# Loading fp32 weights on SyncE's queue with casts on POOL, column sums in bf16 parts, and zero rows beside a half tile

## The chip, the cores and the metric

The kernel runs on one core of one Trainium2 chip. The metric is device time in microseconds (us) of one execution. A "span" is what the profiler saw of one execution; it is about 1.8 us shorter than the device time of the same execution.

## The reference, cut to what matters

```python
B, N, C = 4, 6080, 256                     # q, k, v: (4, 6080, 256) fp32; tau = 1
qn = q / (np.linalg.norm(q, axis=1, keepdims=True) + 1e-6)
kn = k / (np.linalg.norm(k, axis=1, keepdims=True) + 1e-6)
s = kn.transpose(0, 2, 1) @ qn / tau       # (4, 256, 256): one Gram matrix a batch
a = softmax(s)                             # over the last axis
x = (v @ a).reshape(24320, 256)
h = x @ w_in                               # (256, 2048)
return gelu_tanh(h) @ w_out                # (2048, 256)
```

The kernel folds `a @ w_in` into one matrix `aw` a batch, so that each block of 512 tokens needs only `v @ aw`, the gelu, and `@ w_out`.

## The kernel before

Batch 0's attention is computed first (the head). Then 48 blocks of tokens run. Each has 8 slots of four `hp` matmuls (`aw` by transposed v), a gelu on ACT and some `yp` matmuls (`wout`). The attention of the next batch is fed into the slots, a tile of 128 tokens at a time. 6080 tokens are 47 full tiles and a half tile of 64 rows.

The weights are cast by the DMA on POOL's queue, behind a gate that holds them back until a late chunk of k has landed:

```python
# in the head, after the third chunk from the end:
        if n == n_chunks - 3:
            nc.gpsimd.tensor_copy(gate[:, 0:1], st[1][0:1, 0, 0:1])
...
    for c0, c1 in ((0, 1024), (1024, D)):
        nc.gpsimd.dma_start(out=win_bf[:, :, c0:c1], in_=win_v[:, :, c0:c1])
    load_v(1)
    for half in range(2):
        nc.gpsimd.dma_start(out=wout_bf[:, half * 8 : half * 8 + 8, :],
                            in_=wout_v[:, half * 8 : half * 8 + 8, :])
    load_v(2)
```

The Gram matmuls and the sums of squares of the later batches (cut):

```python
            for s, rows in slots_of(ch):             # rows is 64 for the half tile
                first, last = seen == 0, seen == n_all - 1
                gram(G, qk, s, rows, first, last)
                flat = whole[:rows, :, s, :]
                ...                                  # acc (fp32) += flat * flat, on DVE
                yield                                # one slot
                ...
        cols = pA.tile([128, 512], FP32, tag="a", name="cols")
        col_sums(cols, [acc[:, x] for x in range(2)], ones_f, True, True)   # 4 fp32 matmuls
```

Of the kernel before, what the change touches and what calls it, by code (L numbers as in the profile page):

```python
# [8 lines left out]
FP32 = mybir.dt.float32  # L9
BF16 = mybir.dt.bfloat16  # L10
# [8 lines left out]
def kernel(  # L19
# [10 lines left out]
    nc = tc.nc  # L30
    B, N, C = q.shape
    D = moe_w_in.shape[1]
# [8 lines left out]
    REM = N - S_ALL * 128  # L41
# [3 lines left out]
    stage = ctx.enter_context(tc.tile_pool(name="stage", bufs=4))  # L45
# [1 line left out]
    sqp = ctx.enter_context(tc.tile_pool(name="sqp", bufs=3))  # L47
    prp = ctx.enter_context(tc.tile_pool(name="prp", bufs=2))
    sq1 = ctx.enter_context(tc.tile_pool(name="sq1", bufs=4))
    accp = ctx.enter_context(tc.tile_pool(name="accp", bufs=2))  # L50
    smx = ctx.enter_context(tc.tile_pool(name="smx", bufs=2))
    awp = ctx.enter_context(tc.tile_pool(name="awp", bufs=2))
    vts = ctx.enter_context(tc.tile_pool(name="vts", bufs=4))
# [11 lines left out]
    SMAX = 6  # L65
# [11 lines left out]
    def load_chunk(engines, dst, b, chunk, step=1):  # L77

        s0, size, rem = chunk
        for x, src in enumerate((q, k)):  # L80
            engines[x].dma_start(  # L81
                out=dst[x][:, 0:size, :],
                in_=src[b, s0 * 128 : (s0 + size) * 128, :].rearrange("(p s) c -> p s c", s=size))
        if rem:
            for x, src in enumerate((q, k)):
                engines[x].dma_start(out=dst[x][0 : REM * step : step, size, :], in_=src[b, S_ALL * 128 : N, :])

    def slots_of(chunk, rest=REM):
        _, size, rem = chunk
        return [(s, 128) for s in range(size)] + ([(size, rest)] if rem else [])  # L90
# [43 lines left out]
    ones_bf = const.tile([128, 1], BF16)  # L134
    nc.vector.memset(ones_bf, 1.0)
    ones_f = const.tile([128, 1], FP32)
# [3 lines left out]
    gate = const.tile([1, 8], FP32)  # L140
# [3 lines left out]
    win_bf = const.tile([128, 2, D], BF16)  # L144
    wout_bf = const.tile([128, FC, 256], BF16)
    win_v = moe_w_in.rearrange("(c p) d -> p c d", p=128)
# [19 lines left out]
    def col_sums(cols, x, ones, first, last):  # L166

        for m in range(4):
            nc.tensor.matmul(  # L169
                cols[:, m : m + 1],  # L170
                lhsT=x[m // 2][:, m % 2 * 128 : m % 2 * 128 + 128],
                rhs=ones,
                start=first and m == 0,
                stop=last,
                skip_group_check=True,
            )
# [78 lines left out]
    for n, ch in enumerate(first_chunks):  # L255
        st, whole = staged[n]
        size = ch[1]
        qkb, qk_whole = halves(qkp, "qk", BF16, size)
        sqb, sq_whole = halves(sqp, "sq", BF16, size)
        hi = size + ch[2]  # L260
        if whole is None:
            todo = list(zip(qkb, sqb, st))
        else:
            todo = [[y[:, :, 0:hi] for y in (qk_whole, sq_whole, whole)]]
        for to, sq, x in todo:
            nc.vector.tensor_copy(to, x)  # L266
            if n != n_chunks - 2:
                nc.scalar.activation(sq, x, AF.Square)  # L268
        if n == n_chunks - 2:
            nc.scalar.activation(sqb[1][:, 0:hi], st[1][:, 0:hi], AF.Square)  # L270
            nc.vector.tensor_mul(sqb[0][:, 0:hi], qkb[0][:, 0:hi], qkb[0][:, 0:hi])
        keep_clock(fillers[n])
        for s, rows in slots_of(ch, 128):
            gram(G, qkb, s, rows, seen == 0, seen == n_all - 1)
            seen += 1
        if waiting is not None:
            pairs_of(*waiting)
            waiting = None
        if n < 2:
            pairs_of(n, sqb)  # L280
        elif n < TAIL:
            waiting = (n, sqb)
        else:
            sums_of([[y[:rows, s, :] for y in sqb] for s, rows in slots_of(ch, 128)], n == n_chunks - 1)

        for x in ((2, 3) if n == 0 else (4, 5) if n == 1 else (n + 4,)):
            stage_chunk(x)
        if n == n_chunks - 3:
            nc.gpsimd.tensor_copy(gate[:, 0:1], st[1][0:1, 0, 0:1])

    v0 = stage.tile([128, 2, SMAX, 256], FP32, tag="st", name="v0")
    v0 = v0.rearrange("p a b c -> p (a b) c")[:, 0:4, :]
# [10 lines left out]
    def load_v(nb):  # L303
        if nb >= B * n_blocks:
            return
        r0, n, rest = v_parts(nb)
        t = vin.tile([128, 4, 256], BF16, tag="v", name="vb")
        nc.gpsimd.dma_start(  # L308
            out=t[:, 0:n, :],
            in_=v_rows[r0 : r0 + n * 128, :].rearrange("(p s) c -> p s c", s=n))  # L310
        if rest:
            nc.gpsimd.dma_start(out=t[:rest, n, :], in_=v_rows[r0 + n * 128 : r0 + n * 128 + rest, :])
        v_of[nb] = t
# [21 lines left out]
    def load_qk(b, n):  # L335
        if b < B and n < len(later_chunks):
            if at_slot:
                pace()
            t = qkp.tile([128, 2, SMAX, 256], BF16, tag="qk", name="qkb")
            views = [t[:, x] for x in range(2)]  # L340
            load_chunk((nc.gpsimd, nc.gpsimd), views, b, later_chunks[n])
            loaded_of[b, n] = views, t

    for c0, c1 in ((0, 1024), (1024, D)):
        nc.gpsimd.dma_start(out=win_bf[:, :, c0:c1], in_=win_v[:, :, c0:c1])
    load_v(1)
    for half in range(2):
        nc.gpsimd.dma_start(out=wout_bf[:, half * 8 : half * 8 + 8, :],
                            in_=wout_v[:, half * 8 : half * 8 + 8, :])
    load_v(2)  # L350


    r = smx.tile([128, 4], FP32, tag="r", name="r")
# [74 lines left out]
    def attention_steps(b, aw_next):  # L428

        for n in range(16):  # L430
            if n in (3, 9):
                load_qk(b, n // 6)
            if b == 1 and n == 5:
                turn_v_on_pe(1)
            yield
        G = pA.tile([128, 2, 256], FP32, tag="a", name="G")
        acc = accp.tile([128, 2, 256], FP32, tag="acc", name="acc")
        seen = 0
        for n, ch in enumerate(later_chunks):
            load_qk(b, n + 2)  # L440
            qk, whole = loaded_of.pop((b, n))
            for s, rows in slots_of(ch):
                first, last = seen == 0, seen == n_all - 1
                gram(G, qk, s, rows, first, last)
                flat = whole[:rows, :, s, :]
                if first:
                    nc.vector.tensor_mul(acc, flat, flat)
                else:
                    sq = sq1.tile([128, 2, 256], BF16, tag="sq", name="sq")
                    nc.vector.tensor_mul(sq[:rows], flat, flat)  # L450
                    nc.vector.tensor_add(acc[:rows], acc[:rows], sq[:rows])  # L451
                seen += 1
                yield
                if seen % 8 == 0:
                    yield

        cols = pA.tile([128, 512], FP32, tag="a", name="cols")
        col_sums(cols, [acc[:, x] for x in range(2)], ones_f, True, True)
        r = smx.tile([128, 4], FP32, tag="r", name="r")
        nc.vector.tensor_copy(r, cols[:, 0:4])  # L460
        nc.gpsimd.tensor_tensor(r, r, half4, op=ALU.pow)  # L461
        yield
        yield
        yield
        norms(r)
        rh = smx.tile([128, 2], FP32, tag="rh", name="rh")
        nc.vector.tensor_scalar_mul(rh, r[:, 0:2], 0.5)
        Gs = scaled(G, r)
        yield
        yield  # L470
        T = turned(Gs)
        eT = smx.tile([128, 2, 256], BF16, tag="eT", name="eT")
        if abs(inv_tau) > TANH_MAX:
            for jc in range(2):
                nc.scalar.activation(eT[:, jc, :], T[:, jc, :], AF.Exp, scale=r[:, jc : jc + 1])
            yield
        else:
            th = smx.tile([128, 2, 256], FP32, tag="th", name="th")
            den = smx.tile([128, 2, 256], FP32, tag="den", name="den")
            for jc in range(2):  # L480
                nc.scalar.activation(th[:, jc, :], T[:, jc, :], AF.Tanh, scale=rh[:, jc : jc + 1])
            for jc in range(2):
                yield
                nc.vector.tensor_scalar(den[:, jc, :], th[:, jc, :], -1.0, 1.0,
                                        op0=ALU.mult, op1=ALU.add)
                nc.vector.reciprocal(den[:, jc, :], den[:, jc, :])
                nc.vector.scalar_tensor_tensor(
                    out=eT[:, jc, :], in0=th[:, jc, :], scalar=1.0, in1=den[:, jc, :],
                    op0=ALU.add, op1=ALU.mult)
            yield  # L490
            yield
        rsinv = row_sums(eT)
        for fs in range(D // 512):
            for ic in range(2):
                aw_part(eT, rsinv, aw_next, fs, ic)
                yield
# [159 lines left out]
```

## Time and profile before

| | before |
|---|---|
| device time, median of 4 runs | 756.50 us (756.24 to 757.38) |
| span of the profiled run | 754.2 us |
| PE busy | 733.3 us (97%) |
| first `hp` matmul (end of the head) | 41.05 us |
| first `hp` to first Gram matmul of batch 1 | 66.64 - 41.05 = 25.59 us |
| from there to the last `yp` groups | 748.80 - 66.64 = 682.16 us |

The last row comes from the PE timeline. In these views a line is: start in us, length in us, engine, source line, operation, output and inputs, shapes, and in brackets what idle time the engine had before it and what ended it. PE is TensorE and PEld its weight loads, ACT is ScalarE, DVE is VectorE, POOL is GpSimd, SPq is SyncE's queue. `G` is the Gram matrix, `eT` the exponential of its scaled transpose, and `ps` holds `eT` times `win` on its way to `aw`. The prediction shows the lines themselves.

### The profile page before, as it was taken

What the parts mean: (1) busy time and instruction counts of PE and PEld (TensorE: products, weight loads), DVE (VectorE), ACT (ScalarE), POOL (GpSimd) and SP (SyncE); (2) the same over time, 40 slices, a digit from 0 to 9 for tenths busy, and PEclk for the clock granted to TensorE, in tenths of its full rate; (3) what the DMA queues carried; (4) which work ended last, traced back from release to release, by engine and by line L of the source; (5) the groups of instructions that cost most, each with busy time, mean ns of one, the idle gap of its engine ahead of it and who ended that gap; (6) DMA issues with size and microseconds to landing.
All of it is one profiled execution on the core that took longest, in us unless ns stands there. A gap on an engine that the chain in (4) does not pass through costs nothing.

```text
span 754.2 us, 12371 instructions
## 1 busy us (share of the span) xinstructions
PE 733.3 (97%) x5262; PEld 503.5 (67%) x5262; DVE 277.5 (37%) x485; ACT 420.3 (56%) x411; POOL 75.6 (10%) x150
## 2 busy tenths in 40 slices
PE   2999999999999999999999999999999999999998
PEld 1656666776666666776666666766767666666666
DVE  3733556454401546554521265555441011011011
ACT  4875555555456555555555555555546655555552
POOL 1311111101012102101001102010101000000000
PEclk9999999999999999999999999999999999999999
DMA  9999685615147685813435776661513543322111
GB/s 368 346 190 156 103 150 137 118 43 83 48 93 143 114 161 108 162 52 60 99 57 118 140 117 121 148 133 46 83 43 80 96 95 74 69 74 54 41 56 57
DMA packets 79639, 83.59 MB, mean 111 GB/s; under 512 B 55392, under 2 KB 59104, under 8 KB 79072
## 3 DMA queue, kind: packets, MB, share of 16 engines
q0 software_dynamic: 17104, 32.97, 27.4%
q1 hardware_dynamic: 62176, 48.20, 23.8%
q10 hardware_dynamic: 304, 1.64, 0.5%
q8 instruction: 41, 0.67, 0.4%
q14 instruction: 14, 0.11, 0.0%
HBM read 78.91 MB, written 24.90 MB: 138 GB/s over the span
## 4 chain that ended last, share of the span: by engine, by line
PE 94%; DMA 4%; ACT 1%; issue 0%; DVE 0%; SPq 0%; POOL 0%; DVEq 0%
PE yp L510 44%; PE hp L584 44%; PE G L157 4%; PE ps L217 2%; ACT sq L268 1%; DMA st<-in_q_dram 1%; DMA st<-in_k_dram 1%; DMA win_bf<-in_moe_w_in_dram 1%; PE cols L169 0%; PE yp L615 0%; PE T L195 0%; DVE aw L404 0%; PE vps L422 0%; PE ps L384 0%; PE rs L204 0%
## 5 line engine op out<-in xcount | busy, mean ns | idle before, releaser
L588 ACT ACTIVATE g<-hp 128x1024 bf16<-128x1024 f32 (+1 forms) x384 | 389.8, 1015 | 308.2 <-PE hp L584 308.2
L510 PE MATMUL yp<-wout_bf,g 128*128 128x256 bf16 x3024 | 392.0, 273 | 0.0
L584 PE MATMUL hp<-vT,aw 128*128 128x512 bf16 (+1 forms) x1536 | 390.8, 377 | 0.2 <-DVE aw L404 0.2
L510 PEld LDWEIGHTS <-g 128*128 128x128 bf16 x3024 | 295.9, 98 | 113.4
L584 PEld LDWEIGHTS <-aw 128*128 128x128 bf16 x1536 | 149.9, 98 | 104.7 <-issue 0.6
L527 DVE COPY ysb<-yp 128x512 f32<-128x512 f32 (+1 forms) x95 | 64.9, 683 | 402.5 <-PE yp L510 402.5
L451 DVE TENSOR_TENSOR acc<-acc,sq 128x512 f32<-128x512 f32 (+1 forms) x141 | 97.5, 692 | 4.8
L450 DVE TENSOR_TENSOR sq<-qkb 128x512 bf16<-128x512 bf16 (+1 forms) x141 | 58.7, 417 | 0.0
L157 PE MATMUL G<-qkb 128*128 128x256 bf16 (+1 forms) x288 | 55.0, 273 | 0.0
L308 POOL DMA_DIRECT2D vb<-in_v_dram x47 | 25.8, 551 | 76.6 <-DMA vT<-vb 64.3
L226 DVE TENSOR_SCALAR aw<-ps,rsinv 128x512 bf16<-128x512 f32 x30 | 22.4, 749 | 27.1 <-PE ps L217 26.7
L157 PEld LDWEIGHTS <-qkb 128*128 128x128 bf16 (+1 forms) x288 | 27.9, 98 | 3.8 <-issue 0.6
L333 POOL CAST gate<-g 1x1 f32<-1x1 bf16 x24 | 5.9, 244 | 237.3 <-ACT g L588 237.3
L157 PE MATMUL G<-qk 128*128 128x256 bf16 x96 | 13.7, 301 | 15.6 <-DVE qk L266 15.6
L268 ACT ACTIVATE sq<-st 128x3072 bf16<-128x3072 f32 (+2 forms) x9 | 21.1, 2379 | 11.2 <-DMA st<-in_q_dram 8.2
L157 PEld LDWEIGHTS <-qk 128*128 128x128 bf16 x96 | 9.9, 108 | 19.0 <-DVE qk L266 16.6
L266 DVE CAST qk<-st 128x3072 bf16<-128x3072 f32 (+2 forms) x10 | 14.2, 1437 | 13.2 <-DMA st<-in_q_dram 10.0
L217 PE MATMUL ps<-win_bf,eT 128*128 128x512 bf16 x60 | 17.7, 379 | 0.0
L461 POOL TENSOR_TENSOR r<-r,half 128x4 f32<-128x4 f32 x3 | 3.1, 1043 | 113.8 <-DVE r L460 113.8
L81 POOL DMA_DIRECT2D qkb<-in_q_dram x24 | 12.8, 535 | 6.8 <-issue 4.7
L81 POOL DMA_DIRECT2D qkb<-in_k_dram x24 | 12.9, 538 | 0.0
L567 POOL COPY g<-gr 128x1024 bf16<-128x1024 bf16 x2 | 2.1, 1036 | 105.1 <-PE yp L510 105.1
(69 smaller groups left out, 100.7 us busy)
## 6 DMA issues: line engine op xcount, KB each, us to landing
out_dram<-ysb SPq DMA_DIRECT2D x44, 512.0 KB, 2.9
vb<-in_v_dram POOLq DMA_DIRECT2D x43, 256.0 KB, 6.8
qkb<-in_q_dram POOLq DMA_DIRECT2D x21, 384.0 KB, 4.7
qkb<-in_k_dram POOLq DMA_DIRECT2D x21, 384.0 KB, 6.5
st<-in_q_dram SPq DMA_DIRECT2D x2, 1536.0 KB, 11.8
vT<-vb SPq DMA_TRANSPOSE x184, 3.0
st<-in_k_dram ACTq DMA_DIRECT2D x1, 1536.0 KB, 10.3
st<-in_k_dram SPq DMA_DIRECT2D x1, 1536.0 KB, 16.7
```

The lines of the kernel that those rows point to most:

```text
L81: engines[x].dma_start(out=dst[x][:, 0:size, :], in_=src[b, s0 * 128 : (s0 + size) * 128, :].rearrange("(p s) c -> p s c", s=size))
L157: nc.tensor.matmul(G[:, ic, :], lhsT=qk[1][:rows, s, ic * 128 : ic * 128 + 128], rhs=qk[0][:rows, s, :], start=first and ic == 0, stop=las ...
L217: nc.tensor.matmul(ps, lhsT=eT[:, jc, ic * 128 : ic * 128 + 128], rhs=win_bf[:, jc, fs * 512 : fs * 512 + 512], start=jc == 0, stop=jc == 1)
L226: nc.vector.tensor_scalar_mul(dst, ps, scale)
L268: nc.scalar.activation(sq, x, AF.Square)
L308: nc.gpsimd.dma_start(out=t[:, 0:n, :], in_=v_rows[r0 : r0 + n * 128, :].rearrange("(p s) c -> p s c", s=n))
L450: nc.vector.tensor_mul(sq[:rows], flat, flat)
L451: nc.vector.tensor_add(acc[:rows], acc[:rows], sq[:rows])
L510: nc.tensor.matmul(yp[:rows, at, :], lhsT=g[:, fc, s * 128 : s * 128 + rows], rhs=wout_bf[:, fc, :], start=fc == 0, stop=fc == FC - 1)
L527: nc.vector.tensor_copy(ysb[:, s0 : s + 1, :], yp[:, 0 : s + 1 - s0, :])
L584: nc.tensor.matmul(hp[:, j, :cols], lhsT=aw[:, cc, fc * 128 : fc * 128 + 128], rhs=vT[:, cc, :cols], start=cc == 0, stop=cc == 1)
L588: nc.scalar.activation(g[:, 2 * i : 2 * i + 2, :cols], hp[:, :, :cols], AF.Gelu_apprx_tanh)
```

## The change

It has three parts. Weights load as plain fp32 on SyncE's queue and are cast on POOL, to let them start earlier. The sums of squares are split into three bf16 numbers that add up exactly, to avoid fp32 matmuls. The half tile gets zero rows, to make all Gram matmuls the same shape.

```diff
-        if n == n_chunks - 3:
-            nc.gpsimd.tensor_copy(gate[:, 0:1], st[1][0:1, 0, 0:1])
...
+            if later_chunks[n][2]:
+                nc.gpsimd.memset(t[REM:, :, later_chunks[n][1], :], 0.0)
             load_chunk((nc.gpsimd, nc.gpsimd), views, b, later_chunks[n])
...
-    for c0, c1 in ((0, 1024), (1024, D)):
-        nc.gpsimd.dma_start(out=win_bf[:, :, c0:c1], in_=win_v[:, :, c0:c1])
-    load_v(1)
-    for half in range(2):
-        nc.gpsimd.dma_start(out=wout_bf[:, half * 8 : half * 8 + 8, :],
-                            in_=wout_v[:, half * 8 : half * 8 + 8, :])
-    load_v(2)
+    for half in range(2):
+        w = flat_stage(2)                            # a buffer of the q/k staging pool
+        for x in range(2):
+            c0 = half * 1024 + x * 512
+            nc.sync.dma_start(out=w[:, :, x * 512 : x * 512 + 512], in_=win_v[:, :, c0 : c0 + 512])
+            nc.gpsimd.tensor_copy(win_bf[:, :, c0 : c0 + 512], w[:, :, x * 512 : x * 512 + 512])
+        load_v(1 + half)
+    for half in range(2):
+        w = flat_stage(8)
+        nc.sync.dma_start(out=w, in_=wout_v[:, half * 8 : half * 8 + 8, :])
+        nc.gpsimd.tensor_copy(wout_bf[:, half * 8 : half * 8 + 8, :], w)
...
-            for s, rows in slots_of(ch):
+            for s, rows in slots_of(ch, 128):
...
+        parts = [split.tile([128, 2, 256], BF16, tag=f"part{n}", name="part") for n in range(3)]
+        nc.vector.tensor_copy(parts[0], acc)
+        nc.vector.tensor_sub(acc, acc, parts[0])
+        nc.vector.tensor_copy(parts[1], acc)
+        nc.vector.tensor_sub(parts[2], acc, parts[1])
+        yield
+        yield
         cols = pA.tile([128, 512], FP32, tag="a", name="cols")
-        col_sums(cols, [acc[:, x] for x in range(2)], ones_f, True, True)
+        for n, part in enumerate(parts):
+            col_sums(cols, [part[:, x] for x in range(2)], ones_bf, n == 0, n == 2)
```

Left out: the accumulator's pool goes from two buffers to one, and a pool for the parts is added.

More of the change, by code (lines that the diff above doesn't have):

```diff
@@ L49 @@
     sq1 = ctx.enter_context(tc.tile_pool(name="sq1", bufs=4))
-    accp = ctx.enter_context(tc.tile_pool(name="accp", bufs=2))
+    split = ctx.enter_context(tc.tile_pool(name="split", bufs=1))
+    accp = ctx.enter_context(tc.tile_pool(name="accp", bufs=1))
     smx = ctx.enter_context(tc.tile_pool(name="smx", bufs=2))
@@ L340, in load_qk, with flat_stage @@
             views = [t[:, x] for x in range(2)]
+            if later_chunks[n][2]:
+                nc.gpsimd.memset(t[REM:, :, later_chunks[n][1], :], 0.0)
             load_chunk((nc.gpsimd, nc.gpsimd), views, b, later_chunks[n])
             loaded_of[b, n] = views, t
-    for c0, c1 in ((0, 1024), (1024, D)):
-        nc.gpsimd.dma_start(out=win_bf[:, :, c0:c1], in_=win_v[:, :, c0:c1])
-    load_v(1)
+    def flat_stage(n):
+        w = stage.tile([128, 2, SMAX, 256], FP32, tag="st", name="wst")
+        return w.rearrange("p a b c -> p (a b c)")[:, 0:2048].rearrange("p (c d) -> p c d", c=n)
     for half in range(2):
-        nc.gpsimd.dma_start(out=wout_bf[:, half * 8 : half * 8 + 8, :],
-                            in_=wout_v[:, half * 8 : half * 8 + 8, :])
-    load_v(2)
+        w = flat_stage(2)
[8 more added lines that the diff above has]
+        nc.gpsimd.tensor_copy(wout_bf[:, half * 8 : half * 8 + 8, :], w)
     r = smx.tile([128, 4], FP32, tag="r", name="r")
```

## The prediction

> **What bounds the kernel now.** I read the page from the top: span and busy shares, the slices, then the chain of work that ended last.
>
> ```profile
> span 754.2 us, 12371 instructions
> PE 733.3 (97%) x5262; PEld 503.5 (67%) x5262; DVE 277.5 (37%) x485; ACT 420.3 (56%) x411; POOL 75.6 (10%) x150
> PE   2999999999999999999999999999999999999998
> PEclk9999999999999999999999999999999999999999
> PE 94%; DMA 4%; ACT 1%; issue 0%; DVE 0%; SPq 0%; POOL 0%; DVEq 0%
> ```
>
> The reader is to see one full row. PE is busy in every slice but the first and last, its clock is full throughout, and 94% of the chain is PE. The view by stretches says it more sharply: from 50 us to 700 us PE is busy in all of every stretch. So after about 41 us a change can win only by giving PE less to do, and can lose only by making PE wait. Before that, the chain runs through loads: in order of time it is q load, squares, k load, and then this:
>
> ```profile
> 31.83 7.78 DMA win_bf<-in_moe_w_in_dram
> 41.05 1.04 PE hp L584 x4
> ```
>
> The weight load is on the path. The timeline shows by how much:
>
> ```profile
> 38.23 0.84 ACT L374 ACTIVATE eT<-T,r 128x256 bf16<-128x256 f32 x2 [0.50 <-PE T L195]
> 39.74 0.38 PE L384 MATMUL ps<-win_bf,eT 128*128 128x256 bf16 x2 [1.34 <-DMA win_bf<-in_moe_w_in_dram]
> ```
>
> PE idled 1.34 us until win_bf came. Its other operand eT ended at 38.23 + 0.84 = 39.07, so only 39.74 - 39.07 = 0.67 us of that wait belong to the weights.
>
> Two more places in the PE timeline matter, since PE is otherwise full: the half tile (64 rows) and the fp32 column sums.
>
> ```profile
> 74.68 1.03 PE L584 MATMUL hp<-vT,aw 128*128 128x512 bf16 x4
> 75.54 1.04 PE L510 MATMUL yp<-wout_bf,g 128*128 128x256 bf16 x8
> 76.51 0.39 PE L157 MATMUL G<-qkb 64*128 64x256 bf16 x2
> 76.83 1.04 PE L584 MATMUL hp<-vT,aw 128*128 128x512 bf16 x4
> ...
> 170.24 1.04 PE L510 MATMUL yp<-wout_bf,g 128*128 128x256 bf16 x8
> 171.11 0.95 PE L169 MATMUL cols<-ones_f,acc 128*128 128x1 f32 x8
> 171.92 1.02 PE L584 MATMUL hp<-vT,aw 128*128 128x512 bf16 x4
> ```
>
> Starts of successive lines are the thing to compare, because ends are modelled and overlap.
>
> **What the Trainium skill says.** "GPSIMD Engine Reference", section "Elementwise — side-by-side cycle accounting", gives a simple body 1.03 cycles per element at 1.2 GHz. The trace agrees: the POOL copy of 128x1024 bf16 took 1036 ns and the 128x128 fp32-to-bf16 cast 291 ns, so (1036 - 291)/(1024 - 128) = 0.83 ns per element and about 185 ns fixed. "SBUF — State Buffer", section "Who interferes with whom", says that a DVE instruction in a 2-port mode and a POOL instruction exclude each other. The trace fits: the 128x512 fp32 memset at 13.74 took 1072 ns, while DVE was casting until 10.92 + 3.43 = 14.35, against 525 ns for a memset of as many bf16 elements with DVE idle. "DMA: Bandwidth & Descriptors", section "Queues, rings and completion order", says that each DMA engine alternates between the queues with work, packet by packet. Here the rate fell from 371 GB/s in 32 to 34 us to 119 GB/s in 34 to 36, when the software queue's casting loads had joined the tail of v. "TensorE: Matmul & The Clock Gate", section "Weight-path perf modes", says fast weight load is not used for fp32. The trace: 190 ns and two records per fp32 weight load in cols, against 96 ns and one for bf16.
>
> **Part 1, weights.** It removes four casting loads from POOL's queue and the gate that held them until the sixth k chunk (31.71). It adds six plain fp32 loads behind v on SyncE's queue (four of 512 KB, two of 1 MB), and six casts on POOL. The buffers rotate over four: the first weight half takes the one of the fourth chunk, free when its square ends at 25.74 + 2.77 = 28.5. Its loads are therefore queued early and simply follow v. Up to v, 34 us will do for q, k and most of v; I put v at 34.8. At some 0.39 MB per us each 512 KB piece then takes 1.35 us: landings at about 36.1, 37.5, 38.9, 40.2 for win, 42.9 and 45.6 for wout. The casts are 185 + 1024 x 0.83 = 1035 ns and 185 + 2048 x 0.83 = 1.9 us. With the v loads (0.57 us each) in their places on POOL, the casts end at about 37.2, 38.5, 40.1, 41.3, 44.8 and 47.5.
>
> PE wants them, all shifted 0.8 us earlier than now, at: first aw 39.0; second quarter 41.1 (now 41.93); third 42.9 (43.66); fourth 45.5 (46.25); wout's first half 48.0 (48.84), its second two slots later at about 51. Every piece has 1.8 us or more to spare. The v block that PE transposes at 49.27 landed at 33.95 + 10.5 = 44.5 before; now it is issued near 38.5 and may land near 46. It still has 2 us. So the 0.67 us go. The last q and k chunk no longer shares the engines with the casting loads: its square waited 0.25 us for the load and the cast 0.19 us, so I add 0.15. Sum: -0.8 us. The 8.0 us of casts lie on an engine that is idle there.
>
> **Part 2, sums.** It removes, for three batches, the fp32 sums: 171.92 - 171.11 = 0.81 us of PE each; the other two have the same spacing. It adds 12 bf16 pairs each: in the first batch 24 such weight loads took 0.76 us, 0.032 each, so 0.38 us. Saved: 3 x (0.81 - 0.38) = 1.3 us. On DVE it adds four 128x512 operations of at most 0.69 us each (the accumulate's duration), 2.8 us a batch. The accumulator is ready at 168.5, and the sums now come two steps later, at 171.1 + 2 x 1.74 = 174.6, so the split ends 3 us before them. DVE is 37% busy. The two extra steps cost no PE time. One accumulator in place of two costs nothing, since DVE alone now reads and writes it.
>
> **Part 3, zero rows.** The half tile's step, from hp to hp, is 76.83 - 74.68 = 2.15 us; the steps beside it are 1.96 and 1.97. The two added gaps surround the 64-row matmuls, and the weight loads there wait 0.21 us twice for no recorded reason. With 128 rows the step should be like its neighbours: 3 x 0.19 = 0.6 us saved. Each matmul takes 273 ns at either height, so the zeros cost PE nothing. The memset, some 0.5 us on POOL three times, comes ahead of loads that are needed long after.
>
> Sum: -0.8 - 1.3 - 0.6 = -2.7 us, from 756.4: 753.7.
>
> **The rivals.** First, **casts late**. If the 1072 ns memset is fp32's true cost rather than a lock, casts cost 2.1 ns per element, 2.2 and 4.3 us. The same queue then ends the third at 43.1, the fifth near 50 and the sixth near 54.5. PE would stall about 0.2, 2.0 and 1.3 us: 753.7 + 3.5 = 757.2. For it: wout's 1 KB rows may also load slower than q's long ones. Against: the two-point fit above, one of whose points is an fp32 cast. I give it one in seven.
>
> Second, **a lock in the head chain**. The first cast starts near 36.1, just when DVE does its small norm operations (36.24 and 36.53). If one of them has to wait out a 1.03 us cast, the head's 0.8 us is lost: 754.7. For it: the 13.74 memset shows such a wait. Against: DVE's larger operations there read PSUM, and the times must coincide. One in three, so I add 0.3 us to the sum: 754.0.
>
> Third, **the PE savings are illusory**: PE is in order, and a step might be set by another limit, so that cols and gaps hide nothing. Then only the head moves: 755.6. Against: steps without G are shorter by its time (1.74 against 1.96). One in ten.
>
> **Range and chances.** I predict 754.0. The low end, 752.8, has all three savings and a head gain of 1.7. The high end, 756.2, has a late cast that eats most of the gain. A 2% change is 15 us; nothing in the head can bring that, and only a stall in every block could cost it. Faster 0.01, same 0.98, slower 0.01.
>
> **What would show each step.** Right: first aw matmul at 38.6 to 39.1 waiting on eT, not on a weight; POOL casts of 1.0 and 1.9 us ended by 48; the cols group bf16, 36 in all for the three batches, with 0.4 us between their neighbours; no 64-row G and steps of 1.96 there; PE idle nowhere after 41 us. Wrong: PE waiting on POOL's win_bf or wout_bf, a cast above 2 us, or DVE's norm operations lengthened to about 1 us. The prediction fails as a whole if PE shows new idle after 41 us, or if the span falls while PE's steps keep their old spacing.

## The result, and the profile after

The changed kernel took 753.66 us (753.43 to 753.75, 4 runs) against 756.50 us. The ratio is 0.996, with a 95% interval of 0.9943 to 0.9977: "same" at the 2% line.

The page of the changed kernel, busy shares and the chain that ended last:

```profile
span 752.0 us, 12341 instructions
PE 726.4 (97%) x5186; PEld 502.3 (67%) x5274; DVE 284.3 (38%) x497; ACT 420.3 (56%) x411; POOL 80.8 (11%) x154
PE 94%; DMA 3%; ACT 1%; issue 1%; DVE 0%; POOL 0%; SPq 0%; DVEq 0%; POOLq 0%
```

The picture is the same: PE is full. (5186 matmuls recorded against 5274 weight loads: some matmul records are missing from this trace, so PE's busy sum is not compared.) POOL's casts appear, 0% of the chain when rounded, but they are on it. The timeline at the end of the head:

```profile
36.97 1.04 POOL L354 CAST win_bf<-wst 128x1024 bf16<-128x1024 f32 x1 [22.18 <-DMA wst<-in_moe_w_in_dram]
38.08 0.84 ACT L383 ACTIVATE eT<-T,r 128x256 bf16<-128x256 f32 x2 [0.41 <-PE T L196]
38.61 0.39 PE L393 MATMUL ps<-win_bf,eT 128*128 128x256 bf16 x2 [0.35 <-ACT eT L383]
```

The first aw matmul started at 38.61 instead of 39.74, and it waited for eT and no longer for the weights. The first cast took 1.04 us and had ended at 38.01. The first hp matmul came at 40.06, 0.99 us earlier than before. Twelve microseconds later that was gone. The PE timeline near 51 us, first of the changed kernel, then of the kernel before:

```profile
49.88 1.90 POOL L359 CAST wout_bf<-wst 128x2048 bf16<-128x2048 f32 x1 [2.02 <-PE hp L602]
50.09 1.03 PE L602 MATMUL hp<-vT,aw 128*128 128x512 bf16 x4
51.83 0.60 PE L528 MATMUL yp<-wout_bf,g 128*128 128x256 bf16 x4 [0.71 <-POOL wout_bf L359]
```

```profile
51.02 1.03 PE L584 MATMUL hp<-vT,aw 128*128 128x512 bf16 x4
51.88 0.60 PE L510 MATMUL yp<-wout_bf,g 128*128 128x256 bf16 x4
```

Before, yp followed hp by 0.86 us. In the changed kernel it followed by 1.74, because the second half of wout was cast only from 49.88 to 51.78. So 0.88 us were lost here, and 0.06 at the first wout matmul (47.91, 7.85 us after the first hp instead of 7.79). The wait of the cast is put down to a PE matmul, but the cast needs nothing from PE; what it needs is its load, issued at 36.9, which takes 12.9 us to land in the list of issues: 49.8. A wait is put down to the last event that the profile sees, and here that was not the cause. (The issue itself had waited 1.2 us for the staging buffer of v's first block, which PE was transposing. The DMA engines were busy from 34 to 48 us, with shares of 0.99 to 1.12, so an earlier issue would hardly have landed earlier; no run gave wout buffers of its own.)

The steady part, in the places that the prediction shows of before: the former half tile's step, and the column sums.

```profile
74.62 1.03 PE L602 MATMUL hp<-vT,aw 128*128 128x512 bf16 x4
75.48 1.04 PE L528 MATMUL yp<-wout_bf,g 128*128 128x256 bf16 x8
76.36 0.38 PE L158 MATMUL G<-qkb 128*128 128x256 bf16 x2
76.57 1.03 PE L602 MATMUL hp<-vT,aw 128*128 128x512 bf16 x4
...
173.44 1.04 PE L528 MATMUL yp<-wout_bf,g 128*128 128x256 bf16 x8
174.31 0.44 PE L170 MATMUL cols<-ones_bf,part 128*128 128x1 bf16 x12
174.62 0.59 PE L602 MATMUL hp<-vT,aw 128*128 128x512 bf16 x2
```

The step is 76.57 - 74.62 = 1.95 us, like its neighbours, and was 2.15. The column sums hold PE for 174.62 - 174.31 = 0.31 us and did for 0.81.

All traces, cut at the same three points of the PE timeline (us; each is one execution):

| kernel | first hp | to first G | first G to last yp groups | span |
|---|---|---|---|---|
| before | 41.05 | 25.59 | 682.16 | 754.2 |
| changed | 40.06 | 26.52 | 680.01 | 752.0 |
| weights_only | 40.59 | 26.72 | 682.16 | 754.8 |
| sums_only | 42.28 | 26.39 | 680.63 | 754.7 |
| rows_only | 41.55 | 25.59 | 681.52 | 754.1 |
| wout_quarters | 41.34 | 25.58 | 680.01 | 752.4 |
| v2_late | 40.11 | 33.72 | 680.01 | 759.2 |
| wout_long_rows | 40.29 | 26.98 | 680.00 | 752.6 |
| rows_dose | 40.68 | 26.52 | 683.79 | 756.4 |
| one_part | 40.46 | 31.38 | 679.40 | 756.7 |
| after_again (the changed kernel) | 40.38 | 26.69 | 680.01 | 752.5 |
| best | 40.56 | 25.59 | 679.40 | 751.0 |
| win_pieces_sw | 41.71 | 25.58 | 682.16 | 754.9 |
| best_sw | 40.60 | 25.58 | 679.41 | 751.0 |

The last part of an execution repeats to 0.01 us (the changed kernel, wout_quarters, v2_late, wout_long_rows and after_again have the same code there), so differences there can be read from one trace. The head does not: it moves by up to 1.3 us between executions of the same head code. What repeats in the head is its end, from the start of `eT` to the first hp. In all eleven traces in which PE did not wait for win it is 1.97 or 1.98 us (changed: 40.06 - 38.08). In the three with the old win loads it is 2.82 (before: 41.05 - 38.23), 2.68 (rows_only) and 4.15 (sums_only, with a lower clock). So the old loads cost 0.7 us or more in each, 0.84 in the trace of before.

### The profile page after: what moved, and what is told of

The parts are those of the page before. It is cut to its first block, busy times and chain, and to the rows that moved or that the text cites. A ratio compares the mean times of both kernels' runs of the same rounds, so it can differ in the third digit from the quotient of the medians.

```text
span 752.0 us, 12341 instructions
## 1 busy us (share of the span) xinstructions
PE 726.4 (97%) x5186; PEld 502.3 (67%) x5274; DVE 284.3 (38%) x497; ACT 420.3 (56%) x411; POOL 80.8 (11%) x154
## 4 chain that ended last, share of the span: by engine, by line
PE 94%; DMA 3%; ACT 1%; issue 1%; DVE 0%; POOL 0%; SPq 0%; DVEq 0%; POOLq 0%
PE yp L528 44%; PE hp L602 43%; PE G L158 4%; PE ps L218 2%; ACT sq L269 1%; DMA st<-in_q_dram 1%; DMA st<-in_k_dram 1%; PE T L196 0%; POOL wout_bf L359 0%; PE yp L633 0%; PE cols L170 0%; DVE qk L267 0%; DVE aw L413 0%; DVE Gs L188 0%; ACT eT L383 0%
## 5 line engine op out<-in xcount | busy, mean ns | idle before, releaser
L602 PE MATMUL hp<-vT,aw 128*128 128x512 bf16 (+1 forms) x1456 | 383.9, 377 | 3.8 <-DVE aw L413 0.2
L460 DVE TENSOR_TENSOR acc<-acc,sq 128x512 f32<-128x512 f32 x141 | 97.6, 692 | 4.8
L459 DVE TENSOR_TENSOR sq<-qkb 128x512 bf16<-128x512 bf16 x141 | 58.9, 418 | 0.0
L158 PE MATMUL G<-qkb 128*128 128x256 bf16 x288 | 55.0, 273 | 0.0
L158 PEld LDWEIGHTS <-qkb 128*128 128x128 bf16 x288 | 28.2, 98 | 3.3
L82 POOL DMA_DIRECT2D qkb<-in_q_dram x24 | 12.9, 537 | 5.8 <-issue 4.3
L82 POOL DMA_DIRECT2D qkb<-in_k_dram x24 | 12.9, 539 | 0.0
```

Of the source, the lines that this page charges most:

```text
L82: engines[x].dma_start(out=dst[x][:, 0:size, :], in_=src[b, s0 * 128 : (s0 + size) * 128, :].rearrange("(p s) c -> p s c", s=size))
L158: nc.tensor.matmul(G[:, ic, :], lhsT=qk[1][:rows, s, ic * 128 : ic * 128 + 128], rhs=qk[0][:rows, s, :], start=first and ic == 0, stop=las ...
L459: nc.vector.tensor_mul(sq[:rows], flat, flat)
L460: nc.vector.tensor_add(acc[:rows], acc[:rows], sq[:rows])
L602: nc.tensor.matmul(hp[:, j, :cols], lhsT=aw[:, cc, fc * 128 : fc * 128 + 128], rhs=vT[:, cc, :cols], start=cc == 0, stop=cc == 1)
```

## The experiments

The theory after the result: the steady part gained 2.15 us by the sums and the zero rows; the head gained about 1 us and gave it back near 51 us, because wout's second half landed late. Rivals: the head's gain was kept, or the savings on PE were not real. All variants below gave a correct result except wout_long_rows. The times beside `before` are of the same chip and call; the first call's chip was noisier (before: 757.80 us, 756.43 to 759.92, 11 runs; second call 756.67; third call 756.73).

### weights_only: the weight part alone

```diff
 weights_only (before, with)
-            nc.gpsimd.tensor_copy(gate[:, 0:1], st[1][0:1, 0, 0:1])
-        nc.gpsimd.dma_start(out=win_bf[:, :, c0:c1], in_=win_v[:, :, c0:c1])
-        nc.gpsimd.dma_start(out=wout_bf[:, half * 8 : half * 8 + 8, :], ...)
+            nc.sync.dma_start(out=w[...], in_=win_v[...])      # four pieces of win
+            nc.gpsimd.tensor_copy(win_bf[...], w[...])
+        nc.sync.dma_start(out=w, in_=wout_v[...])              # two pieces of wout
+        nc.gpsimd.tensor_copy(wout_bf[...], w)
```

> The kernel before with the weight part alone. Theory (the head gains about 1 us and PE then loses about 0.9 us waiting for the second half of wout): the first hp matmul near 40.1 instead of 41.05, a PE wait of about 0.7 us on POOL's wout_bf near 51, the first G matmul within 0.2 us of 66.64, span 754.0 to 754.3, time the same as before within 0.2 us. Rival (the prediction as written, head gain kept): first G near 65.8, span 753.4, time 0.8 us shorter.

Measured: 756.32 us, ratio 0.9982 (0.9969 to 0.9995). In the trace the first hp came at 40.59 and PE again waited for wout's cast:

```profile
50.55 1.03 PE L590 MATMUL hp<-vT,aw 128*128 128x512 bf16 x4
52.56 0.60 PE L516 MATMUL yp<-wout_bf,g 128*128 128x256 bf16 x4 [0.98 <-POOL wout_bf L356]
```

The first G came at 67.31, later than in the trace of before; I had said within 0.2 us of 66.64, so that number was missed by 0.5. The span of 754.8 was missed too, and so was the time: 1.48 us below before in the medians, where the theories had at most 0.8. The mechanism is there: the stretch from first hp to first G is 26.72, 1.13 longer than before, and the steady part is unchanged to the last digit. By this trace the weight part brings nothing. Yet the six timed runs are 0.18% faster than before. In part the traces mislead: weights_only's is its slowest run (756.62 us), and that of before (756.02) is faster than all but two of its 35 timed runs. What else differs is under "the granted clock" below.

### sums_only and rows_only: the other two parts alone

```diff
 sums_only (before, with)
+        parts = [...]   # three bf16 parts of acc, two yields, as in the change
-        col_sums(cols, [acc[:, x] for x in range(2)], ones_f, True, True)
+        for n, part in enumerate(parts):
+            col_sums(cols, [part[:, x] for x in range(2)], ones_bf, n == 0, n == 2)
 rows_only (before, with)
+                nc.gpsimd.memset(t[REM:, :, later_chunks[n][1], :], 0.0)
-            for s, rows in slots_of(ch):
+            for s, rows in slots_of(ch, 128):
```

> The kernel before with the bf16 sums alone. Theory: cols group to next hp 0.31 us instead of 0.81, three times, so 1.5 us: span 752.7. Prediction as written: 0.38 us and 1.3 us, span 752.9. Rival (PE savings illusory, the step is set elsewhere): span 754.2.

> The kernel before with the zero rows alone. Theory: the half tile's step is 1.96 us instead of 2.15, three times, 0.6 us: span 753.6, and no weight load with a wait of 0.21 us around it. Rival (illusory): span 754.2.

Measured: sums_only 756.02 us, ratio 0.9973 (0.9956 to 0.9989); rows_only 756.10 us, ratio 0.9984 (0.9969 to 1.0). The spans (754.7 and 754.1) are above what I expected, both because of the head, where these two have the old weight loads: their first hp came at 42.28 and 41.55. In the steady part, which is what they change, sums_only is 682.16 - 680.63 = 1.53 us shorter and rows_only 682.16 - 681.52 = 0.64. Together that is 2.17, and the changed kernel has 2.15. The savings on PE are real, they add up, and the rival is out.

The trace of sums_only shows a second thing. PE waited longer for the old weight load, and the granted clock (1.00 is TensorE's full speed) fell after it. From the PE timeline, and from the view by stretches (length, busy time of each engine with counts, then granted clock, DMA share and GB/s):

```profile
40.52 0.59 PE L385 MATMUL ps<-win_bf,eT 128*128 128x256 bf16 x2 [2.21 <-DMA win_bf<-in_moe_w_in_dram]
```

```profile
36.00:40.00 4.00, 1.79 (x13) 1.13 (x12) 1.91 (x5) 2.93 (x6) 1.50 (x3) 1.00 1.01 159
40.00:50.00 10.00, 9.48 (x44) 4.65 (x45) 5.23 (x9) 6.28 (x8) 0.17 (x1) 0.83 1.27 198
```

Over 10 us the mean clock was 0.83, which is 1.7 us of full-speed work; the trace of before has 1.00 there.

### wout_quarters: the same bytes in smaller pieces

```diff
 (changed kernel, with)
         w = flat_stage(8)
-        nc.sync.dma_start(out=w, in_=wout_v[:, half * 8 : half * 8 + 8, :])
-        nc.gpsimd.tensor_copy(wout_bf[:, half * 8 : half * 8 + 8, :], w)
+        for x in range(2):
+            t0 = half * 8 + x * 4
+            nc.sync.dma_start(out=w[:, x * 4 : x * 4 + 4, :], in_=wout_v[:, t0 : t0 + 4, :])
+            nc.gpsimd.tensor_copy(wout_bf[:, t0 : t0 + 4, :], w[:, x * 4 : x * 4 + 4, :])
```

> The changed kernel with wout loaded and cast in four pieces of 512 KB instead of two of 1 MB. Theory (PE waits near 51 because the 1 MB piece lands whole at 49.8 and is then cast whole in 1.9 us): the piece that PE wants at 51 lands by about 48 and is cast by 49.5, no PE wait on wout_bf, first G near 65.7 instead of 66.58, span 751.1, 0.9 us less than the changed kernel. Rival (the transfers as such are too late, whatever the piece): the wait stays above 0.5 us and the span at 752.

Measured: 753.48 us, ratio 0.9948 (0.9933 to 0.9963). No PE wait for wout_bf is left in the list of waits, and the stretch from first hp to first G is 25.58 us, as before the change. The third piece was cast from 48.10 to 49.14, as expected. The span was 752.4 and not 751.1, because in this execution the clock was 0.83 between 20 and 30 us and the head ended at 41.34; three of the six timed runs had spans of 751.1. So the wait was removed as theory said, and the head's own scatter hid it in the profiled run.

### v2_late and wout_long_rows: why wout landed late

The prediction had wout's halves landing at 42.9 and 45.6. The changed kernel began to cast them at 45.96 and 49.88, as soon as they were there. Two suspects: the loads of the v blocks share the DMA engines, and each row of wout is only 1 KB.

```diff
 v2_late (changed kernel, with)
-        load_v(1 + half)
+        if half == 0:
+            load_v(1)
...                                     # the two wout loads and casts
+    load_v(2)
 wout_long_rows (changed kernel, with; wrong result on purpose)
+    wout_long = moe_w_out.rearrange("(p t) d -> p t d", p=128)
-        nc.sync.dma_start(out=w, in_=wout_v[:, half * 8 : half * 8 + 8, :])
+        nc.sync.dma_start(out=w, in_=wout_long[:, half * 8 : half * 8 + 8, :])
```

> The changed kernel with the load of the third v block (512 KB read) issued after the wout casts instead of before them. Theory A (wout lands late because the v loads, left out of the prediction's bytes, share the DMA engines): wout's halves land about 1.3 us earlier, the second near 48.5 instead of 49.8, its cast ends by 50.5 and the PE wait of 0.7 us is gone; span about 751.1. Theory B (wout lands late because its rows of 1 KB load slowly): second half still lands after 49.4 and PE still waits; span 752.

> The changed kernel with wout read in another row order, so that each partition gets 8 KB in one run instead of eight rows of 1 KB. The result is wrong on purpose; only time counts. Theory B (short rows are slow): second half lands 1.5 us or more earlier and PE no longer waits. Theory A (bytes shared with v): landing within 0.4 us of 49.8 and the wait stays.

The casts of wout (count, shortest/median/longest in ns, first and last start in us), first of v2_late, then of wout_long_rows:

```profile
L360 POOL CAST wout_bf<-wst x2: 1896/1896/1896, 45.1 to 48.8; 128x2048 bf16<-128x2048 f32 x2
```

```profile
L361 POOL CAST wout_bf<-wst x2: 1896/1896/1897, 43.7 to 47.3; 128x2048 bf16<-128x2048 f32 x2
```

Both suspects were right, in unequal parts. Without v's third block beside it, the second half came 49.88 - 48.81 = 1.07 us earlier; with long rows 49.88 - 47.30 = 2.58 us earlier. Three further traces with the changed weight part had that cast at 50.4 to 50.6, so the differences are not smaller than this. The long rows also change the addresses that are read, which no run separates from their length. In both variants PE's wait for wout was gone.

Both were slower all the same: v2_late 762.05 us, ratio 1.0078 (1.0057 to 1.01), and wout_long_rows 754.38 us, 0.9969 (0.9954 to 0.9984), no better than the changed kernel. From the PE timeline of v2_late:

```profile
63.30 0.82 PE L530 MATMUL yp<-wout_bf,g 128*128 128x256 bf16 x6
70.48 1.87 PE L604 MATMUL hp<-vT,aw 128*128 128x512 bf16 x4 [6.36 <-DMA vT<-vb]
```

The edit treats the third v block as a load with time to spare, since its matmuls come at 65 us. What I forgot is the step between: four DMA transposes. In the changed kernel they started at 48.90; the first two took 2.4 and 2.3 us to land, the third 6.1, and the last one, issued at 52.8, took 8.7: 61.5, with 3.3 us to spare. In v2_late they started at 54.35, and the last, issued at 59.1, took 11.2 us: 70.3. PE idled 6.4 us, and the clock was 0.85 from 60 to 70 us and 0.81 from 70 to 80. In wout_long_rows the v block was in time (48.58), but POOL was free earlier, so the next batch's q and k loads were issued from 50.38 instead of 52.95. The last transpose took 12.8 us from 52.6, and PE waited 1.2 us at 65.53. That the q and k loads slowed the transposes is read from these times; no run took them away. It would mean that an engine off the path had set when a transfer started, and so what it collided with.

### rows_dose: more matmuls of 64 rows

```diff
 (changed kernel, with; drops rows on purpose)
-                gram(G, qk, s, rows, first, last)
+                gram(G, qk, s, 64 if s == 2 and n < 6 else rows, first, last)
```

> The changed kernel with the Gram matmuls of 18 full tiles (six a batch, each alone in its step) cut to 64 rows. The result is wrong on purpose. Theory (a change of the row count between neighbouring matmuls costs about 0.1 us each way, whatever the tile): 18 x 0.19 = 3.5 us more, span 755.5, each such step 2.15 us, the weight load after each with a wait of about 0.2 us. Rival (the old gap came from the half tile's own loads or operands): span 752.0.

Measured: 758.20 us, ratio 1.0014 (1.0001 to 1.0027). (The result is not the reference's, but with these inputs the comparison still passed.) The steady part grew by 683.79 - 680.01 = 3.78 us, or 0.21 us for each of the 18 steps. The weight loads around one of them:

```profile
71.20 0.11 PEld L158 LDWEIGHTS <-qkb 64*128 64x128 bf16 x2 [0.21 <-issue]
71.52 0.55 PEld L602 LDWEIGHTS <-aw 128*128 128x128 bf16 x4 [0.21 <-issue]
```

The two waits of 0.21 us that stood around the half tile now stand around full tiles that were cut. So the row count costs, and not this tile. One wait stands before the pair and one after it, which fits a cost of each change; that a 64-row pair costs as such, among its like too, was not ruled out, since every pair here stood alone.

### one_part: three edits at once

```diff
 (changed kernel with wout in four pieces, load_v(2) after them, and)
         nc.vector.tensor_copy(parts[0], acc)
-        nc.vector.tensor_sub(acc, acc, parts[0])
-        nc.vector.tensor_copy(parts[1], acc)
-        nc.vector.tensor_sub(parts[2], acc, parts[1])
         ...                            # and one part instead of three in col_sums
```

> The changed kernel with wout in four pieces, the third v block's load after them, and the sums of squares as one bf16 number instead of three (no longer exact; each square was already rounded to bf16). Theory: 4 instead of 12 pairs, 8 x 0.026 = 0.2 us less in each of three batches, and no wait on wout: 0.9 + 0.6 = 1.5 us less than the changed kernel, span 750.5, still within the tolerance. Rival (pairs that few are bound by something else): span 751.1, the gain of wout alone.

Measured: 760.91 us, ratio 1.0045 (1.0031 to 1.0059). It failed by the same late v load as v2_late (PE waited 4.3 us for vT). The sums alone did what was expected: 680.01 - 679.40 = 0.61 us less in the steady part, 0.20 a batch for 8 pairs, 0.025 us a pair. The result is still correct; the split into three parts is exact, but these inputs don't need it.

### after_again, best, win_pieces_sw, best_sw

The changed kernel beside a better one, and whether the new queue was needed at all:

```diff
 best (changed kernel, with load_v(2) left in place, and)
+        for x in range(2):                    # wout in four pieces, as in wout_quarters
-        nc.vector.tensor_sub(acc, acc, parts[0])
-        nc.vector.tensor_copy(parts[1], acc)
-        nc.vector.tensor_sub(parts[2], acc, parts[1])   # one part, as in one_part
 win_pieces_sw (before, with)
-    for c0, c1 in ((0, 1024), (1024, D)):
+    for c0, c1 in ((0, 512), (512, 1024), (1024, 1536), (1536, D)):
         nc.gpsimd.dma_start(out=win_bf[:, :, c0:c1], in_=win_v[:, :, c0:c1])
 best_sw (win_pieces_sw, with the zero rows and the sums in one part)
```

> The changed kernel once more, beside the three others of this call. From the first G matmul to the first of the last column matmuls 680.0 us, from the first hp to the first G 26.5, a PE wait on POOL's wout_bf of 0.7 to 1.0 us. Only the start of the first aw matmul should vary, by up to 1.3 us, as it did over the runs so far.

> The changed kernel with wout in four pieces and the sums of squares as one bf16 number, the third v block's load left where it was. Theory: from the first hp to the first G 25.58 us (no wait on wout, none on the transposed v), from there to the last columns 679.4, together 1.55 us less than the changed kernel of the same call. Rival (the pieces push v's transposes late, as the moved v load did): PE waits for vT near 65.

> The kernel before with win still cast by the DMA from POOL's queue behind the gate, but in four pieces of 512 columns instead of two of 1024. Theory P (the head waited because the first piece was large): the first aw matmul waits for eT, not for win, 0.7 to 1 us earlier, and no wait on wout follows; span 0.8 us less than before. Theory Q (the head waited because the gated queue of POOL starts late and moves slowly): PE still waits for win_bf by 0.6 us or more and the span is within 0.3 us of before.

> The kernel before with win in four pieces as in the run just above, the zero rows, and the sums as one bf16 number. Theory P: everything that the changed kernel gains on PE (2.15 + 0.6 = 2.75 us from the first G on) and a head as early, with no wait on wout: as fast as the best kernel of this call within 0.4 us. Theory Q: the same PE gain, head as before: about 1 us slower than it.

| kernel | median us (lowest to highest, 5 runs) | ratio to before | interval |
|---|---|---|---|
| after_again | 753.98 (753.29 to 754.35) | 0.9960 | 0.9947 to 0.9972 |
| best | 753.03 (752.51 to 753.98) | 0.9949 | 0.9936 to 0.9961 |
| win_pieces_sw | 755.74 (755.51 to 756.64) | 0.9986 | 0.9973 to 0.9998 |
| best_sw | 753.08 (752.82 to 753.58) | 0.9951 | 0.9937 to 0.9964 |

The changed kernel repeats: 0.9960 as in the first comparison. In the trace of best the list of all PE waits is this (total us, times, longest):

```profile
PE G L158 <- DVE qk L267: 16.1, 4, 14.3
PE T L196 <- DVE Gs L188: 0.4, 1, 0.4
PE ps L395 <- ACT eT L385: 0.4, 1, 0.4
PE hp L601 <- DVE aw L415: 0.2, 1, 0.2
```

All lie in the head; the last one, of 0.2 us, is that of the first hp itself, and after it PE waits for nothing. The two later stretches are (26.69 - 25.59) + (680.01 - 679.40) = 1.71 us shorter than in after_again, against 1.55 expected. Medians differ by 0.95; the intervals of the two ratios overlap, so the timed runs alone would not settle it, and the traces do.

win_pieces_sw is the instructive one. It keeps the old queue, the old gate and the casting DMA:

```profile
40.26 0.39 PE L384 MATMUL ps<-win_bf,eT 128*128 128x256 bf16 x2 [0.35 <-ACT eT L374]
```

PE waits for eT, as in the changed kernel, and no wait for wout follows (25.58 us to the first G). The span that theory P expected was missed (754.9, against 754.2 before), because eT itself was late: it started at 39.73, with a clock of 0.83 from 20 to 30 us, and the first hp came 1.98 us after it, as in the changed kernel. The timed runs are 0.99 us below before in their medians. So theory P holds for the wait: the first piece of win was too large, and the queue mattered little. best_sw, with the old queue, is as fast as best.

### The granted clock, from all timed runs

Every run lists the mean granted clock of its span. Of 31 runs of before, 19 had a clock below 0.999, and took 757.67 us on the mean; the other 12 took 756.49 on the mean. Of the 9 runs of the changed kernel (both times) none had it, and they took 753.79. sums_only and rows_only, which keep the old win loads, had it in 4 and 3 of 6 runs; weights_only in none of 6, wout_quarters in 3 of 6, wout_long_rows and rows_dose in 1 of 4 each, best and win_pieces_sw in 1 of 5 each, best_sw in none of 5. (v2_late and one_part had it in every run; their PE waited for vT.) So it is 26 of 43 runs with the two large win loads and 7 of 44 without. A PE wait for win long enough to lower the clock, as in the trace of sums_only, fits this. It is not shown for the runs of before, which were timed without a trace of their own. And there is a rival: in the traces of wout_quarters and win_pieces_sw the dip (0.83) lies between 20 and 30 us, before any weight is wanted. If the first account holds, the weight part's worth is some 1.2 us in more than half of the runs of before, about 0.7 us on the mean, and not the head's gain that I had in mind.

## Why the prediction was right

The total was right: 754.0 predicted, 753.66 measured. Two of its three terms had the mechanism right, and one was right only by accident. By its own test it fared worse: it was to fail "as a whole if PE shows new idle after 41 us", and PE did show 0.71 us of it, before the yp matmul at 51.83. That was also one of its signs of being wrong, PE waiting on POOL's wout_bf, with a cast that ended at 51.78 instead of by 48.

**Part 2, sums.** Predicted 1.3 us, measured alone 1.53. The mechanism was right; the term "0.032 each, so 0.38 us" for 12 pairs was mis-sized. It measured 0.31. The 0.76 us was the length of a group, with the whole of its last instruction in it, and not a spacing of starts, which the prediction itself says is the thing to compare: PE's 24 matmuls there took 0.74 us, which is 23 x 0.025 + 0.163, and in the steady part too a further pair costs 0.025 us (one_part). The four DVE operations took 0.43, 0.69, 0.43 and 0.69 us and ended 3.7 us before the sums. They cost nothing, as predicted.

**Part 3, zero rows.** Predicted 0.6 us, measured alone 0.64; and rows_dose shows that the row count is the cause. The 0.5 us memset (520 ns) held up nothing on PE: rows_only shows no PE wait after the head.

**Part 1, weights.** Here the steps failed and the sum was lucky. "So the 0.67 us go" was too small: of the 0.99 us by which the first hp moved, 0.84 lie after the start of eT, since the first aw matmuls need only the first half of eT, which ends near 38.7 and not at 39.07. "Every piece has 1.8 us or more to spare" was wrong: the wout landings "42.9 and 45.6" left out the bytes of the two v blocks and took rows of 1 KB to load like rows of many KB. The runs put 1.07 us on one v block and 2.58 us on the rows, of some 4.2 us; the two were not tried together. Some 1.5 us of the 4.2 were there before wout: win's casts began at 36.97, 38.31, 40.35 and 41.69 against landings I put at 36.1, 37.5, 38.9 and 40.2. The second v block, whose load was issued at 39.30, may be part of that; no run moved it. So 0.93 us of the head's gain were given back near 51 us, and the net in the two traces is 41.05 + 25.59 - 40.06 - 26.52 = 0.06 us. The added 0.15 us came, for the most part from elsewhere: eT started 0.15 us earlier, but only 0.06 of it were there at the square of the last chunk. The other 0.09 are the first norm operation (see the second rival). Both are small beside the 1.3 us by which heads differ.

**The rivals.** "Casts late" came true in its outcome and not in its reason. The casts took 1.04 and 1.90 us, as worked out, and not 2.2 and 4.3; their loads were late. The prediction names the 1 KB rows there as a point for it, and then gives them no time. "A lock in the head chain" did not occur: the norm operations took 0.17 and 0.18 us at 36.18 and 36.39, and the first cast began at 36.97. They never met in a trace, so what a cast would have done is left open. But such a lock was in the kernel before, where nobody looked:

```profile
34.50 2.00 POOL L348 DMA_DIRECT2D wout_bf<-in_moe_w_out_dram  x2
36.24 0.26 DVE L180 TENSOR_SCALAR r<-r 128x4 f32<-128x4 f32 x1 [1.09 <-ACT r L354]
```

The norm operation took 0.26 us here and ended at 36.50, with POOL's issue of the wout load. In sums_only and rows_only it took 0.25 us and in best_sw 0.56, each time until a POOL issue ended, to 0.01 us; in the ten other traces it took 0.17 us. That the issue holds DVE up is read from this coincidence; no run isolates it. "Savings illusory" fell with sums_only and rows_only. (The sum has a slip too: for the second rival 753.7 + 0.8 would be 754.5, while 754.7 adds the whole cast, and of the three rivals only this one was weighed into the 754.0.)

What made the sum right: the spans differ by 2.2 us, 2.15 of it in the steady part, and the timed runs by 2.84 in their medians. Of the rest, 0.48 us is that the profiled run of before (756.02 us) was faster than its median. Why its other runs are longer is not shown; the clock dips, which nobody had reckoned with, fit.

## What to carry to other kernels

When one engine is full, count what it does between two of its own starts, at the places where shape or type changes: a lone 64-row matmul pair cost 0.2 us more than one of 128 rows, and four fp32 sums 0.8 us, and the two savings add up to within 0.02 us (2.17 alone, 2.15 together). A load that gates a full engine should first be cut to the piece that is needed first; that did for the head here what a new queue and six casts did. Before moving a load later, follow its data through every step to its reader: the v block "with time to spare" had four slow transposes in front of it and cost 6.4 us.

## What the Trainium skill lacked or had wrong

- "TensorEngine Tiling (Array Packing)", section "Key Properties", says that changing the tiling mode drains TensorE, but gives no number. Here a 64-row pair among 128-row matmuls cost 0.19 us in the kernel before and 0.21 us in each of 18 steps of rows_dose.
- "TensorE: Matmul & The Clock Gate", Part 3, section "The mechanism", says that a weight load overlaps a running matmul only when the row group differs. Here loads of the same 128 rows overlapped (from 100 to 150 us of before PE was busy for 50.00 us and its weight loads for 34.90; the same section's other clause, a background weight buffer, would cover that), and those with another row count waited 0.21 us.
- "DMA: Bandwidth & Descriptors", section "Specifications", puts the smallest transfer for line rate at 512 B. The wout load in 1 KB rows had its second half 2.6 us later than in 8 KB runs (2 MB in all, with other loads beside it, and with other addresses).
- "FP8 and Floating Point Precision", section "TensorE Precision Notes", has fp32 at four passes. The trace has two records per fp32 matmul (24 for 12; how many passes a record holds it does not tell), and four such matmuls with one column held PE for 0.81 us, against 0.11 us for four in bf16 (in the trace of best, 173.88 to 173.99).
- No page that I read has how DMA transposes slow down beside other loads: in the changed kernel the four of one block took 2.4, 2.3, 6.1 and 8.7 us from issue to landing, the later ones with the q and k loads (issued from 52.95) in flight, and the last took 11.2 and 12.8 us in the two variants in which those loads were issued before it.
